# Attention scores and value products as full-precision small tiles inside a fused attention and MLP kernel

## The chip, the cores and the metric

The kernel runs on one core of one Trainium2 chip. The metric is the time of one execution on the device in microseconds (us). A run of it is some hundreds of microseconds of one program on five engines: PE (matmul; PEld is its weight load), DVE, ACT, POOL, and SP, which here only issues DMAs.

## What is computed

Attention with keys and values averaged over groups of 8 positions, then a two-layer MLP with a rational activation. 8 batches x 8 heads x 576 queries x 64; so 72 pooled keys for each head, 4608 tokens, 512 model columns, 2048 hidden columns, all float32:

```python
k_p = k.reshape(B, H, Sp, 8, D).mean(axis=3);  v_p = v.reshape(B, H, Sp, 8, D).mean(axis=3)
scores = scale * np.matmul(q, k_p.transpose(0, 1, 3, 2))
attn = softmax(scores)                               # over the 72 pooled keys
x = np.matmul(attn, v_p)  ->  (4608, 512)
h = x @ w_in;  g = P(h) / (Q(h) + 1e-6)              # cubic over quadratic, by element
out = g @ w_out
```

## The kernel before

**Blocks.** The tokens go through in 13 blocks: blocks 0 to 2 of 256 tokens ("short", `i < SHORT`) and 3 to 12 of 384 ("late"). 128 tokens are one tile `t`. A block of 384 lies in one batch (7 of the ten) or crosses from one batch into the next (3); `segs` gives its pieces.

**Attention of a block** (`attend`, L847). `squares` brings `q` in; `attention` (L712) runs once for each `t`: it makes `qT`, multiplies it by the pooled keys `kpT` into the scores `ps` (two PSUM banks), subtracts the maximum, takes the exponential on ACT, the sum on DVE, and normalises on POOL. The keys of the two heads of a pair stand block-diagonally in `kpT` (zeros elsewhere), so that one full-size product has 144 columns, two heads of 72. These products are in full float32, which PE runs as two records each. Where a tile crosses into another batch, its products are 64 output columns wide, alternately in the two halves of the array (`128*64` in the rows). The weights are then turned so that keys lie on partitions: in the short blocks by PE into `pm` and `pr`, in the late ones by 32x32 squares on DVE and 16 DMAs for each block (`am<-e`). Since the 144 keys of two heads don't fit in 128 partitions, the first 16 go separately (`rem`, `four`).

**Values** (`values`, L798). The turned weights are split into a high part `hi` and a rest `lo` (tile `am`), the pooled values into `vm` (high, rest) and `vr` (`split_v`, L664). For each of 4 head pairs and each piece of the block there are four products in the faster reduced type float32r; the result `pv` is copied to `x` as high part and rest.

**MLP.** `mm1` (L906) makes a hidden slice `ph` by 12 products of 384 columns, `rational` computes the activation on ACT, DVE and POOL (5 DVE and 6 ACT passes for each slice) into `gh` and `gl`, `mm2` (L967) adds 9 products of 512 columns into the output banks `po`, three for a late block. So PE alternates `ph` and `po`, and PSUM's 8 banks are shared by `po`, `ph`, the activation's `rp`, `ps` and `pv`.

**What sets the order.** Nothing is issued as it is written. Every call is recorded as an `Op` with a planner's own cost (`Plan.add`), given a due time, shifted by the table `LATER` (operation number to microseconds), and `Plan.solve` (L199) lays the operations on the engines, the earliest start first and, within `LOOK` of it, the earliest due. `Plan.issue` (L297) emits that order; all instructions of the plan therefore have the line L339. Where the plan leaves PE idle early on, it adds filler matmuls (L330): 512 columns into `idle` up to a marked operation, 256 columns of zeros into the next operation's own bank after it.

Of the kernel before, what the change touches and what calls it, by code (L numbers as in the profile page):

```python
# [101 lines left out]
class Op:  # L102
    __slots__ = ("eng", "cost", "port", "calls", "deps", "users", "bufs", "due", "wait",
                 "ready", "seq", "bytes", "early", "slack", "start", "end", "done", "lead", "keep",
                 "spare")


class Plan:
# [8 lines left out]
    LOOK = 0.02  # L117
# [21 lines left out]
    }  # L139
    HOLD = {}  # L140

# [13 lines left out]
    def add(self, eng, cost, calls, port=False, claims=(), bytes=0, early=40.0, after=()):  # L155
        op = Op()
        op.eng, op.cost, op.port, op.calls, op.bytes = eng, cost, port, calls, bytes
        op.early, op.slack, op.lead = early, self.slack, 0.0
        op.keep, op.spare = self.keep, 0
# [39 lines left out]
    def solve(self):  # L199
# [14 lines left out]
        port = bus = 0.0  # L214
        flights = [0.0] * 8
        done, order = 0, []
        while done < len(self.ops):
            best = None
            for e, cands in engs.items():
                pick = None  # L220
                opts = []
                for op in cands:
                    t = max(at[e], op.ready)
# [46 lines left out]
            at[op.eng] = op.end  # L270
            if op.port:
                port = op.end
# [24 lines left out]
    def issue(self):  # L297
# [8 lines left out]
        for op in self.order:  # L306
            if op.eng == "pe":
# [8 lines left out]
                else:  # L316
                    to = None
                    own = op.calls[0][1][0]
                    if own.tile.it is None and free is not None and op.start < self.HEAD_END:
                        to, one, first = own.tile.real(), self.zeros, True  # L320
                        to = to.rearrange("p a b -> p (a b)") if len(own.tile.shape) > 2 else to
                        to = to[:, 0:256] if op.start - free > 0.5 else None
# [35 lines left out]
def tile_pooled_attention_then_rational_moe(  # L358
# [24 lines left out]
    REM = 2 * SP - P  # L383
# [29 lines left out]
    pool("work4", 3)  # L413
# [14 lines left out]
    def pe(ns, calls, claims=(), after=()):  # L428
        return plan.add("pe", ns / 1000, calls, claims=claims, after=after)
# [23 lines left out]
    masks = new("cpool", "masks", [P, 6], F32, "masks")  # L453

    spread = new("work1", "vs", [P, 3 * P], F32, "fourfold")
    fourfold, line, ab = spread[:2 * REM, 0:P], spread[0:1, P:2 * P], spread[0:1, 2 * P:2 * P + 6]
    bands = new("cpool", "bands", [P, 4], F32, "bands")

    mlo, mhi = masks[:, 0:1], masks[:, 1:2]

    mrem_lo, mrem = ([masks[:, i + m:i + m + 1] for m in range(2)] for i in (2, 4))
# [6 lines left out]
    def make_masks():  # L468
        def band(m, lo, hi):

            small("memset", m, 1.0 / G)
            if lo > 0:
                small("affine_select", out=m, in_=m, pattern=[[0, 1]], compare_op=ALU.is_ge,
                      fill=0.0, base=-lo, channel_multiplier=1)
            if hi < P:
                small("affine_select", out=m, in_=m, pattern=[[0, 1]], compare_op=ALU.is_ge,
                      fill=0.0, base=hi - 1, channel_multiplier=-1)
# [11 lines left out]

# [644 lines left out]
```

## Time and profile before

| | |
|---|---|
| three runs | 883.92, 886.62, 886.92 us |
| median | 886.62 us |
| span of the profiled execution | 882.1 us |
| PE busy | 865.0 us, 98% |
| DVE, ACT, POOL busy | 770.0 (87%), 725.3 (82%), 549.7 us (62%) |
| matmuls of the MLP (`ph`, `po`) | 3936 of 5056 PE records |

The span reaches from the first to the last instruction; the median of the runs is 4.5 us above it. A PE record's duration includes the way through the array, which overlaps with the next record, so a cost is read as the distance between the starts of two groups, not as the duration of one.

### The profile page before, as it was taken

The numbers are of one execution on the slowest core, as the hardware profiler recorded it, in microseconds if no ns is written. First come the engines' busy times: TensorE is split into PE (matmuls) and PEld (weight loads), VectorE is DVE, ScalarE is ACT, GpSimd is POOL, SyncE is SP. The second block draws the span as 40 slices with busy tenths as digits, with TensorE's granted clock in tenths as the row PEclk, the third lists the DMA queues.
The fourth block names the chain that finished last, engine by engine and source line by source line (L and its number), as shares of the span: only waits on it lengthen the run. The fifth ranks groups of instructions, "written<-read, shape, count | busy, mean of one in ns | idle before, by whom it ended". The sixth has DMA issues, their size and how long they took to land.

```text
span 882.1 us, 15805 instructions
## 1 busy us (share of the span) xinstructions
PE 865.0 (98%) x5056; PEld 802.3 (91%) x5056; DVE 770.0 (87%) x1585; ACT 725.3 (82%) x1373; POOL 549.7 (62%) x614
## 2 busy tenths in 40 slices
PE   8899989999999999999999999999999999999998
PEld 7799879898999999999999999999999999999997
DVE  6899987878998988988998987998998987997764
ACT  4798898987688788788798797788888888888886
POOL 5767779786646744666655854646655764554554
PEclk9999999999999999999999999999999999999999
DMA  9896651133344232144034142043232432030000
GB/s 297 203 391 239 166 128 47 37 121 108 79 117 110 43 80 60 30 93 129 15 77 101 30 87 36 37 84 75 94 54 50 113 54 38 37 49 6 37 1 36
DMA packets 192919, 79.17 MB, mean 90 GB/s; under 512 B 169412, under 2 KB 169412, under 8 KB 192836
## 3 DMA queue, kind: packets, MB, share of 16 engines
q1 hardware_dynamic: 192836, 78.16, 34.1%
q8 instruction: 40, 0.66, 0.3%
q14 instruction: 43, 0.35, 0.1%
HBM read 52.17 MB, written 14.16 MB: 75 GB/s over the span
## 4 chain that ended last, share of the span: by engine, by line
PE 75%; ACT 9%; DMA 4%; DVE 4%; POOL 3%; SPq 2%; issue 2%; POOLq 0%; DVEq 0%; ACTq 0%
PE po L339 35%; PE ph L339 34%; PE ps L339 3%; PE pv L339 3%; SPq L339 2%; DMA rwin<-in_moe_w_in_dram 2%; DMA q<-in_q_dram 2%; ACT rp L339 1%; DVE t L339 1%; ACT r L339 1%; ACT t L339 1%; POOL gl L339 1%; ACT gh L339 1%; ACT hi L339 1%; ACT m_wout L339 1%
## 5 line engine op out<-in xcount | busy, mean ns | idle before, releaser
L339 PE MATMUL ph<-x,win 128*128 128x384 f32 (+1 forms) x2208 | 379.5, 320 | 1.2 <-POOL win L339 0.6
L339 PEld LDWEIGHTS ph<-x,win 128*128 128x128 f32 x2208 | 356.4, 189 | 12.2 <-PE po L339 0.9
L339 PE MATMUL po<-wout,gh 128*128 128x512 f32 x1152 | 300.2, 383 | 4.9 <-ACT gh L339 4.4
L339 POOL TENSOR_TENSOR w<-w,r 128x384 f32<-128x384 f32 (+2 forms) x186 | 196.3, 1056 | 148.2 <-ACT r L339 137.5
L339 POOL TENSOR_TENSOR gl<-t,gh 128x384 fp32r<-128x384 f32 (+2 forms) x186 | 201.3, 1084 | 127.4 <-ACT gh L339 89.5
L339 PEld LDWEIGHTS po<-wout,gh 128*128 128x128 f32 x1152 | 209.3, 189 | 29.9 <-ACT gh L339 6.5
L339 DVE SCALAR_TENSOR_TENSOR t<-t,abn,rp 128x384 f32<-128x384 f32 (+2 forms) x186 | 115.0, 620 | 58.8 <-ACT rp L339 57.6
L339 PE MATMUL po<-wout,gl 128*128 128x512 f32 x576 | 162.0, 382 | 0.7 <-POOL gl L339 0.7
L339 ACT ACTIVATE t<-ph,abn 128x384 f32<-128x384 f32 (+2 forms) x186 | 125.9, 678 | 35.2 <-DVE rp L339 13.0
L339 ACT ACTIVATE r<-w,abn 128x384 f32<-128x384 f32 (+2 forms) x186 | 133.0, 715 | 9.2 <-POOL gl L339 4.3
L339 ACT ACTIVATE rp<-w,cbias 128x384 f32<-128x384 f32 (+2 forms) x186 | 110.5, 594 | 30.8 <-POOL w L339 25.7
L339 DVE TENSOR_TENSOR t<-t,ph 128x384 f32<-128x384 f32 (+2 forms) x186 | 104.0, 560 | 19.3 <-ACT w L339 10.4
L339 PEld LDWEIGHTS po<-wout,gl 128*128 128x128 f32 x576 | 104.6, 189 | 12.4 <-POOL gl L339 2.1
L339 DVE SCALAR_TENSOR_TENSOR t<-t,abn,ph 128x384 f32<-128x384 f32 (+2 forms) x186 | 114.8, 618 | 1.2
L339 ACT ACTIVATE w<-ph 128x384 f32<-128x384 f32 (+2 forms) x186 | 92.3, 496 | 22.0 <-PE ph L339 17.6
L339 ACT CAST gh<-t 128x384 fp32r<-128x384 f32 (+2 forms) x186 | 95.9, 516 | 14.7 <-DVE t L339 9.7
L339 DVE SCALAR_TENSOR_TENSOR t<-rp,t 128x384 f32<-128x384 f32 (+2 forms) x186 | 104.4, 561 | 1.9
L339 DVE SCALAR_TENSOR_TENSOR rp<-w,rp 128x384 f32<-128x384 f32 (+2 forms) x186 | 105.2, 566 | 0.0
L339 ACT ACTIVATE rp<-rp 128x384 f32<-128x384 f32 (+2 forms) x186 | 91.0, 490 | 2.2
L339 POOL TENSOR_TENSOR e<-e,sm 128x576 f32<-128x576 f32 x36 | 42.9, 1203 | 29.8 <-DVE sm L339 28.7
L339 POOL TENSOR_TENSOR st_v<-st_v 128x256 f32<-128x256 f32 (+1 forms) x72 | 42.2, 596 | 7.5 <-DMA st_v<-in_v_dram 4.6
L339 PE MATMUL ps<-kpT,qT 128*128 128x144 f32 (+1 forms) x304 | 41.6, 290 | 0.3 <-DVE qT L339 0.3
(116 smaller groups left out, 876.2 us busy)
## 6 DMA issues: line engine op xcount, KB each, us to landing
am<-e SPq DMA_DIRECT2D x160, 72.0 KB, 2.4
rwin<-in_moe_w_in_dram SPq DMA_DIRECT2D x8, 1024.0 KB, 8.4
rwout<-in_moe_w_out_dram SPq DMA_DIRECT2D x8, 1024.0 KB, 11.6
out_dram<-ob SPq DMA_DIRECT2D x30, 256.0 KB, 2.5
st_k<-in_k_dram SPq DMA_DIRECT2D x24, 256.0 KB, 3.2
st_v<-in_v_dram SPq DMA_DIRECT2D x24, 256.0 KB, 2.7
q<-in_q_dram SPq DMA_DIRECT2D x112, 48.0 KB, 2.1
xd<-x SPq DMA_DIRECT2D x6, 512.0 KB, 13.8
```

Source lines behind the costliest of these rows:

```text
L339: getattr(engines[op.eng], name)(*map(value, args), **{k: value(v) for k, v in kw.items()})
```

## The change

The score products take 64 rows and 64 output columns each, one head and 64 tokens, over 72 keys; four of them stand in the four quarters of the array, the two heads of a pair in different row halves and different PSUM banks. The value products take 32 keys and 64 output columns: four head pairs in four row groups and four banks, two heads in two column halves. Both are full float32, two records each. Weights and values are no longer split (`hi`, `lo`, `vm`, `vr` are gone). Short blocks turn their weights by float32 products with the identity, 32 output columns wide, instead of PE's transpose. Late blocks are handled whole: one `attention_all` with 48 score products into four banks, 24 or 48 value products into four banks. The planner gets a switching cost `DRAIN` between kinds of PE tile (`mode`), a rule that holds PSUM banks for an operation that needs more than two (`waits`, `room`), a `LOOK` of 0.3, and a new `LATER` table of some 430 entries.

```diff
-    LOOK = 0.02
+    LOOK = 0.3
     LATER = {
-        83: -4, 85: -17, 95: 2, 105: -1, 119: 4, 139: 27, 172: 1, 196: 5, 290: 5, 332: 2, 355: 10,
...
+        1: 20, 4: -810, 9: -530, 14: -380, 25: -380, 26: -40, 27: -210, 28: -70, 29: -210,
...
+    DRAIN = 0.18
...
+            wide = min((op for op in engs["pe"] if op.due <= at["pe"] + self.SOON
+                        and op.ready <= at["pe"] + self.AHEAD and op.waits()),
+                       key=lambda op: op.due, default=None)
+            room = wide and sum(b.ring.tag == "ps" for b in wide.bufs)
...
+                    t = max(at[e] + (self.DRAIN if e == "pe" and op.mode != mode else 0.0),
+                            op.ready)
...
+                                if wide and op is not wide and not mine[0].sum:
+                                    n += room
...
-    pool("work4", 3)
+    pool("work4", 4)
...
     def prep_v_early(n):
+        for r in range(4):
+            for hh in range(2):
+                rows = v[n, 2 * r:2 * r + 2].rearrange("h (s t) d -> (h s) (t d)", t=G)
+                dma(128, early(n, 2)[r * HB:(r + 1) * HB].rearrange(
+                    "p (c h x) -> p c h x", c=2, h=2)[:, :, hh],
+                    rows[WINDOWS[hh]:WINDOWS[hh] + 2 * HB].rearrange("(c k) x -> k c x", c=2))
-        dma(1024, st, rows[:, REM:, :].rearrange("j r x -> r j x"))
...
+    def scores(i, out, qT, ms):
+        calls = []
+        for m in ms:
+            for j in range(NJ):
+                for ch in range(2):
+                    n = (tok0(i) + m * P + ch * D) // S
+                    for hh in range(2):
+                        rows = slice(hh * D, (hh + 1) * D)
+                        o = out(hh, m, j)
+                        calls.append(mm(o.tile_at(slice(ch * D, (ch + 1) * D)), qT(rows, m, j, ch),
+                                        kpT[n % 2][rows, j, :], True, True))
+        return calls
...
+            return [mm(o(r), pairs[:, r, WINDOWS[u]:WINDOWS[u] + HB], ident, True, True)
+                    for r in range(4)]
+        pe(232 * 4, [x for u in range(4) for x in turned(
+            lambda r: pm[r * HB:(r + 1) * HB, u, :], u)], claims=(mt,), mode=3)
...
+    def attention_all(i, mt, qs, es):
+        dve(NJ * size(i)).transpose(qs, qs)
+        cut = 512 // SP
+        parts = ((0, cut), (cut, NQ))
+        ps = [[bank(f"ps{i}_{hh}{x}", [P, q1 - q0, SP]) for x, (q0, q1) in enumerate(parts)]
+              for hh in range(2)]
+        pe(127 * NQ, every, claims=(es, mx, sm), mode=1)
+        for x, (q0, q1) in enumerate(parts):
+            for hh in range(2):
+                k = q1 - q0
+                dve(k * SP).tensor_reduce(out=mx[:, hh, q0:q1], in_=ps[hh][x], op=ALU.max,
+                                          axis=AX.X)
+                dve(k * SP).tensor_tensor(
+                    out=es[:, q0:q1, hh], in0=ps[hh][x],
+                    in1=mx[:, hh, q0:q1].unsqueeze(2).to_broadcast([P, k, SP]), op=ALU.subtract)
...
-                    terms = ((o, vh[:, j, :], h), (o, vl[:, j, :], h),
-                             (pv[:D, jj, r0:r1], vr[b % 2][:, j, :], rest),
-                             (o, vh[:, j, :], l))
...
+        pv = [bank(f"pv{i}_{r}", [P, n]) for r in range(4)]
+        for r0, r1, b in segs(tok0(i), n):
+            w = vw[b % 2]
+            for c in range(3):
+                for r in range(4):
+                    rows = slice(r * HB, r * HB + (HB if c < 2 else 2 * LAST))
+                    for hh in range(2):
+                        calls.append(mm(pv[r][hh * D:(hh + 1) * D, r0:r1], w[rows, 2 * c + hh],
+                                        mt[rows, 2 * c + hh if c < 2 else 4, r0:r1],
+                                        c == 0, c == 2))
+        pe(cost, calls, claims=[x_at(xs, 0, j)[0] for j in (0, 2)], mode=2)
```

How the order moves is shown at three places. In the rows, `ps_0_4377` is a bank `ps` and its number; x2 means two such instructions in a row.

First, PE at the scores of late block 6, before; `po` belongs to the block that is in the MLP at that time:

```order
L339 MATMUL po_0_2_3544<-wout_2498,gl_7_1_4319 128x512
L339 MATMUL ps_0_4377<-kpT_184,qT_4293 128x144 x2
L339 MATMUL po_0_0_4384<-wout_752,gh_0_0_4348 128x512
L339 MATMUL po_0_1_4388<-wout_752,gh_0_0_4348 128x512
L339 MATMUL po_0_2_4394<-wout_752,gh_0_0_4348 128x512
L339 MATMUL po_0_0_4384<-wout_752,gh_0_0_4348 128x512
L339 MATMUL ps_1_4400<-kpT_184,qT_4293 128x144 x2
```

and in the changed kernel, the start of the same block's scores:

```order
L397 MATMUL po_0_2_3692<-wout_2580,gl_7_0_4474 128x512
L397 MATMUL po_0_0_3677<-wout_2580,gh_7_1_4492 128x512
L397 MATMUL po_0_1_3681<-wout_2580,gh_7_1_4492 128x512
L397 MATMUL po_0_2_3692<-wout_2580,gh_7_1_4492 128x512
L397 MATMUL ps_00_4516<-kpT_592,q_4335 64x72
L397 MATMUL ps_10_4518<-kpT_592,q_4335 64x72
```

Twelve products in six or fewer groups among the `po` became 48 small ones in one group, into four banks (`ps_00`, `ps_10`, `ps_01`, `ps_11`); `po` matmuls stand on both sides.

Second, DVE behind those scores, before:

```order
L339 TENSOR_REDUCE mx_4390<-ps_0_4377 128x4
L339 SCALAR_TENSOR_TENSOR t_1_1_4301<-rp_1_1_4352,t_1_1_4301 128x384
L339 TENSOR_TENSOR e_4406<-ps_0_4377,mx_4390 128x2x144
L339 TENSOR_TENSOR t_2_0_4339<-t_2_0_4339,ph_2_0_4286 128x384
L339 TENSOR_REDUCE mx_4390<-ps_1_4400 128x4
```

and in the changed kernel (`t` and `rp` are the activation's tiles, `mx` and `e` the attention's, `ob` the output copy):

```order
L397 SCALAR_TENSOR_TENSOR t_1_1_4505<-t_1_1_4505,abn,ph_1_1_4442 128x384
L397 TENSOR_REDUCE mx_4578<-ps_00_4516 128x7
L397 TENSOR_REDUCE mx_4578<-ps_10_4518 128x7
L397 TENSOR_SCALAR ob_7_0_4584<-po_0_0_3677 128x512
L397 TENSOR_REDUCE mx_4578<-ps_01_4546 128x5
L397 TENSOR_REDUCE mx_4578<-ps_11_4548 128x5
L397 TENSOR_TENSOR e_4611<-ps_00_4516,mx_4578 128x7x72
L397 TENSOR_TENSOR e_4611<-ps_10_4518,mx_4578 128x7x72
L397 TENSOR_TENSOR e_4611<-ps_01_4546,mx_4578 128x5x72
L397 TENSOR_TENSOR e_4611<-ps_11_4548,mx_4578 128x5x72
L397 SCALAR_TENSOR_TENSOR t_1_0_4456<-t_1_0_4456,abn,rp_1_0_4575 128x384
```

The passes over the scores stood one by one between passes of the activation; now eight of them and one output copy stand in a row.

Third, PE in the opening, at the turning of block 1's weights, before:

```order
L339 MATMUL ps_1_495<-kpT_102,early_1_208 128x144 x2
L339 MATMUL ph_1_0_478<-x_385,win_460 128x256 x20
L330 MATMUL pm_575<-zero,identr 128x256 x23
L339 MATMUL pm_575<-identr,e_472 128x128 x4
L339 MATMUL pq_606<-identr,q_476 128x128 x4
```

and in the changed kernel (line L388 emits its fillers):

```order
L388 MATMUL idle<-identr 128x512 x5
L397 MATMUL ph_2_0_505<-x_398,win_480 128x256 x16
L388 MATMUL idle<-identr 128x512
L397 MATMUL pl_639<-identr,ks_166 128x128
L397 MATMUL ph_2_0_505<-x_398,win_480 128x256 x4
L397 MATMUL idle<-identr 128x128
L388 MATMUL pm_683<-zero,identr 128x256 x48
L397 MATMUL pm_683<-identr,e_558 32x128 x16
```

The place has 48 filler matmuls of zeros where it had 23, and the 512-column fillers, which ended earlier, now reach up to it. Over the program the 512-column fillers go from 23 to 54 and those of 256 columns from 47 to 48.

## Rows read from the trace of the kernel before

**Rows 1.** The page: span, busy time by engine, granted TensorE clock in 40 slices (tenths).

```profile
span 882.1 us, 15805 instructions
...
PE 865.0 (98%) x5056; PEld 802.3 (91%) x5056; DVE 770.0 (87%) x1585; ACT 725.3 (82%) x1373; POOL 549.7 (62%) x614
...
PEclk9999999999999999999999999999999999999999
```

**Rows 2.** Busy time by stretch; columns as its first line says.

```profile
core 0: us, PE busy (x) PEld busy (x) DVE busy (x) ACT busy (x) POOL busy (x), PEclk, DMA share, GB/s
0.00:50.00 50.00, 43.78 (x307) 38.30 (x308) 38.55 (x81) 31.30 (x59) 32.59 (x71) 1.00 0.91 266
50.00:100.00 50.00, 48.83 (x354) 45.38 (x353) 49.76 (x96) 42.98 (x68) 34.25 (x22) 1.00 0.75 277
300.00:500.00 200.00, 199.79 (x1132) 186.94 (x1131) 183.61 (x398) 166.38 (x331) 119.74 (x139) 1.00 0.31 70
500.00:700.00 200.00, 199.60 (x1118) 185.77 (x1118) 179.47 (x389) 165.74 (x328) 116.70 (x129) 1.00 0.31 67
```

**Rows 3.** Order of time on PE, late, a tile in two batches: start us, us, instructions.

```profile
692.08 0.38 PE L339 MATMUL po<-wout,gl 128*128 128x512 f32 x1
692.39 1.20 PE L339 MATMUL ps<-kpT,qT 128*64 128x144 f32 x16
693.52 0.48 PE L339 MATMUL po<-wout,gl 128*128 128x512 f32 x1
693.84 0.38 PE L339 MATMUL po<-wout,gh 128*128 128x512 f32 x1
```

**Rows 4.** The same view in the opening: fillers, scores of a whole tile, transposes.

```profile
2.52 4.43 PE L330 MATMUL idle<-identr 128*128 128x512 f32 x10
...
11.43 1.14 PE L339 MATMUL ps<-kpT,early 128*128 128x144 f32 x8
12.41 3.62 PE L339 MATMUL pvs<-early,identr 128*128 128x256 f32 x16
...
37.75 2.74 PE L330 MATMUL pm<-zero,identr 128*128 128x256 f32 x23
...
43.83 0.60 PE L339 MATMUL pm<-identr,e 128*128 128x128 f32 x4
44.27 0.38 PE L339 MATMUL pr<-identr,e 128*128 128x128 f32 x2
```

**Rows 5.** The same view at values, block in one batch.

```profile
388.81 0.49 PE L339 MATMUL pv<-hi,vm 128*128 128x384 f32 x2
...
389.46 0.81 PE L339 MATMUL po<-wout,gh 128*128 128x512 f32 x3
```

**Rows 6.** The same view at values, block in two batches; between them 31 more.

```profile
526.41 0.81 PE L339 MATMUL po<-wout,gl 128*128 128x512 f32 x3
527.06 0.36 PE L339 MATMUL pv<-hi,vm 128*128 128x192 f32 x2
...
530.42 1.26 PE L339 MATMUL po<-wout,gh 128*128 128x512 f32 x5
```

**Rows 7.** Groups on DVE by form: count, busy us, mean ns, idle before.

```profile
L339 DVE TENSOR_REDUCE mx<-ps 128x4 f32<-128x288 f32 x72 | 30.8, 438 | 2.0 <-PE ps L339 1.8
L339 DVE TENSOR_TENSOR e<-ps,mx 128x288 f32<-128x288 f32 x72 | 29.8, 443 | 0.1
L339 DVE TENSOR_TENSOR x<-pv,x 128x384 fp32r<-128x384 f32 x40 | 21.2, 552 | 4.5 <-ACT x L339 4.0
...
L339 DVE TENSOR_TENSOR am<-am,hi 128x768 fp32r<-128x768 f32 x20 | 19.7, 997 | 0.7 <-ACT hi L339 0.2
...
L339 DVE TENSOR_SCALAR ob<-po 128x512 f32<-128x512 f32 x13 | 8.9, 686 | 2.9 <-PE po L339 2.7
```

**Rows 8.** Groups on ACT by form, the same columns.

```profile
L339 ACT CAST x<-pv 128x384 fp32r<-128x384 f32 x40 | 18.0, 480 | 2.1 <-PE pv L339 2.0
L339 ACT CAST hi<-am 128x768 fp32r<-128x768 f32 x20 | 16.3, 830 | 0.1
```

More of the change, by code (lines that the diff above doesn't have):

```diff
@@ L104, with waits @@
                  "ready", "seq", "bytes", "early", "slack", "start", "end", "done", "lead", "keep",
-                 "spare")
+                 "spare", "mode")
+    def waits(self):
+        out = [b for b in self.bufs if not b.held]
+        return sum(b.ring.tag == "ps" for b in out) > 2 and all(
+            len(b.ring.free) >= sum(x.ring is b.ring for x in out) and b in b.ring.queue[:2]
+            for b in out if b.ring.tag != "ps")
 class Plan:
@@ L452, in tile_pooled_attention_then_rational_moe @@
     zero = real([P, 1], F32R, tag="zero", name="zero")
[L453 to L461, printed above, removed]
+    line = new("work1", "vs", [P, 3 * P], F32, "line")
+    line, ab = line[0:1, 0:P], line[0:1, 2 * P:2 * P + 6]
+    masks = new("cpool", "masks", [P, 2], F32, "masks")
+    mlast = [masks[:, m:m + 1] for m in range(2)]
     QC = 1.0 + 1e-6
@@ L596, in prep_k @@
             if n < 2 or c1 == 5:
-                turned = pe(109 * len(turns_), turns_)
+                turned = pe(109 * len(turns_), turns_,
+                            after=[o for o, _ in kpT[n % 2].tile.reads])
                 turned.lead = 1.5 if n > 2 else 0.0
@@ L664, in split_v @@
[L664 to L680 removed]
+        place = early(n, 1)[:, CW:CW + RW]
@@ L710, in squares, with __init__, tile_at, attention @@
         return qs
-    def attention(i, m, hi, lo, qs, es):
+    def scores(i, out, qT, ms):
[10 more added lines that the diff above has]
+        return calls
+    class Part:
+        def __init__(self, bank_, at):
+            self.bank, self.at = bank_, at
+        def tile_at(self, rows):
+            return self.bank[rows, self.at, :]
+    def attention(i, m, mt, qs, es):
         t = tok0(i) // P + m
@@ L738, in attention @@
-        pairs = es[:, :, m]
-        e = es[:, 0:NJ, m].rearrange("p j (h s) -> p j h s", s=SP)
-        mx = new("work2", "mx", [P, H], F32, f"mx{t}")
-        sm = new("work2", "sm", [P, H], F32, f"sm{t}")
-        scores = [bank(f"ps{t}_{c}", [P, 4, SP]) for c in range(2)]
-        calls = [mm(scores[c][r0:r1, 2 * jj:2 * jj + 2, :], qT[:, 2 * c + jj, r0:r1],
-                    kpT[n % 2][:, 2 * c + jj, :], True, True)
-                 for c in range(2) for jj in range(2) for r0, r1, n in sg]
@@ L758, in attention @@
-        ef = es[:, 0:NJ, m]
-        act(H * SP + 24).activation(ef, ef, AF.Exp, scale=D ** -0.5)
-        dve(H * SP).tensor_reduce(out=sm.rearrange("p (j h) -> p j h", h=2), in_=e, op=ALU.add,
-                                  axis=AX.X)
+        j0 = m * (NJ // 2)
+        qt = qs[:, j0:j0 + NJ // 2].rearrange("p a b (c d) -> p (a b c d)", d=HB).rearrange(
+            "p (h d) -> p h d", d=D)
+        for r0, r1, n in sg:
+            s0 = t * P + r0 - n * S
+            dma(2 * (r1 - r0), qt[r0:r1],
+                q[n, :, s0:s0 + (r1 - r0), :].rearrange("h s d -> s h d"), run=256)
@@ new lines, in attention @@
+        pq = bank(f"pq{t}", [P, NJ, P])
+        pe(110 * NJ, [
+            ("transpose", (pq[:, j, :],
+                           qt[:, 2 * j:2 * j + 2, :].rearrange("s h d -> s (h d)"), ident),
+             {}) for j in range(NJ)], claims=(qT,))
+        act(NJ * P).copy(qT, pq)
+        e = es[:, m]
+        mx = new("work2", "mx", [P, 2, NJ], F32, f"mx{t}")
+        sm = new("work2", "sm", [P, H], F32, f"sm{t}")
+        ps = [bank(f"ps{t}_{hh}", [P, NJ, SP]) for hh in range(2)]
+        pe(127 * NJ, scores(i, lambda hh, m, j: Part(ps[hh], j),
+                            lambda rows, m, j, ch: qT[rows, j, ch * D:(ch + 1) * D], [m]),
+           claims=(e, mx, sm), mode=1)
@@ new lines, in attention @@
+        for hh in range(2):
+            dve(4 * SP).tensor_reduce(out=mx[:, hh], in_=ps[hh], op=ALU.max, axis=AX.X)
+            dve(4 * SP).tensor_tensor(
+                out=es[:, m, :, hh], in0=ps[hh],
+                in1=mx[:, hh].unsqueeze(2).to_broadcast([P, NJ, SP]), op=ALU.subtract)
+        act(H * SP + 24).activation(e, e, AF.Exp, scale=D ** -0.5)
+        normal(e.rearrange("p j h s -> p (j h) s"), sm, H * SP)
+        pm = bank(f"pm{t}", [P, 4, P])
+        pr = bank(f"pr{t}", [P, P])
@@ L843, in x_at @@
         return tile, idx if c is None else (idx[0], c, *idx[1:])
-    prepared, shared = set(), {}
+    prepared = set()
     def attend(i):
@@ L1060, in due @@
         return HEAD + SLOW * min(at, SLOWS) + PACE * max(0, at - SLOWS)
-    for i in range(2):
-        plan.add("pool", 0.5, [("memset", (kpT[i], 0.0), {})], port=True)
     plan.idle = bank("idle", [P, 4, P])
@@ L1069, in tile_pooled_attention_then_rational_moe @@
     plan.now = 0.0
-    for g in range(4):
-        small("tensor_copy", out=fourfold[:, g * 32:(g + 1) * 32], in_=ident[:2 * REM, :2 * REM])
     make_masks()
```

304 lines of the change are left out of this document (102 added, 202 removed), and 62 rows, old and new, of the table LATER.

## The prediction

> **What bounds the kernel now.** I read the page first: PE is busy 98% of 882.1 us and its clock is granted in full in every slice [rows 1], so the question is whether PE waits anywhere and what it spends on attention. By stretches [rows 2] there are two regimes. In the first 100 us PE is busy 43.78 and 48.83 of 50 us, that is 7.4 us idle, although it also runs fillers that produce nothing; there the DMA engines are busy for 91% and 75%. From 300 to 700 us PE idles 0.6 of 400 us: every microsecond of PE work taken out there comes off the end, and nothing that relieves another engine can bring anything, because nothing keeps PE waiting. DVE is next with 363 of the same 400 us, so it may become the bound if it is handled badly. Second view: the order of time on PE, read start to start [rows 3 to 6], since a record's duration overlaps with the next.
>
> **Paces.** A full-width score tile has 8 records from 11.43 to 12.41 us, 0.1225 us each [rows 4]; with 144 columns that is 0.85 ns a column in full float32. A `po` record of 512 columns takes 0.216 us (three from 526.41 to 527.06 [rows 6]), 0.42 ns a column in float32r: full precision costs twice. A tile in two batches already uses half-width products, alternately in the two column halves [rows 3]: 16 records in 1.20 us. The last record's own way is 0.28 us (1.14 less 7 spacings of 0.1225 [rows 4]), so 15 spacings take 0.92 us, 0.061 us each, half the full-width spacing: two tiles do run side by side. The price stands at both ends. `po` at 692.08 would have let the array go at 692.30, and the next regular rhythm begins at 693.84 - 0.216 = 693.62; that is 1.33 us for 16 records which need 0.98. An excursion into small tiles costs 0.35 us.
>
> **Late blocks, scores.** Now: 3 tiles x 0.98 = 2.94 us a block, and 0.35 more in the three blocks with a tile in two batches. Then: 48 products, 96 records, four side by side, is 24 sets of 72 columns x 0.85 ns = 0.061 us, 1.47 us, and one excursion: 1.82. Saved: 7 x 1.12 + 3 x 1.47 = 12.2 us.
>
> **Late blocks, values.** Now 0.65 us a head pair (388.81 to 389.46 [rows 5]), 2.60 a block in one batch, and 3.36 in two (527.06 to 530.42 [rows 6]). Then 24 products, 48 records, eight side by side: 6 sets x 384 x 0.85 ns = 1.96 us, or 12 sets of 192 columns, also 1.96, and an excursion: 2.31. Saved: 7 x 0.29 + 3 x 1.05 = 5.2 us. That row groups work side by side like column halves is not in this trace; I take it so for now and price the contrary below. Together the late blocks give **-17.4 us**, all on the path by the 0.6 us idle [rows 2].
>
> **Late blocks, other engines.** The split of the weights goes: two passes of 997 ns and a half-height one on DVE, copies of 830 ns on ACT for each block [rows 7, 8]. The normalised weights go out in 16 DMAs as before, a sixth smaller. Since PE does not wait there, I cost all this at nothing; it is slack for the last rival.
>
> **Short blocks.** Six score tiles: from 5 x 0.98 + 1.33 = 6.2 us to 6 x (0.49 + 0.35) = 5.0, -1.2. Turning the weights: 36 records at 0.11 us (four from 43.83 to 44.27 [rows 4]), 4.0 us, become 240 float32 records, four side by side, 60 x 128 x 0.85 ns = 6.5 us, and five excursions, 1.75: +4.3. The values of three blocks change by less than a microsecond and are left out. The net is +3.1 us.
>
> **Fillers.** The order has 31 more of 512 columns. Four more stand in the first group, which runs at 0.44 us each (ten in 4.43 us [rows 4]); 27 at 0.216; that is 7.6 us. The zeros of 256 columns go from 47 to 48, at 0.12 us (23 in 2.74 us [rows 4]), no term, but 48 of them now stand in one place. Fillers stand where the plan expects PE to wait. If they only cover the 7.4 us that PE idles in the first 100 us [rows 2], they cost nothing; if all of that idle stays, they cost 7.6. Neither row is nearer, so I take half, +3.8, and keep both ends. The value loads of batches 0 and 1 become 12 DMAs each instead of 3; four of the first eight, 0.5 MB, stand ahead of the first `q`, 2 us at 266 GB/s [rows 2]. I hold that within the fillers' term.
>
> **Sum.** -17.4 + 3.1 + 3.8 = -10.5 us. This is made against the profiled execution of 882.1 us and carried to the median of the runs, 886.62, which lies 4.5 above it: **876 us**. Its own range is 868 (fillers free, cheaper excursions, since neighbouring ones share an end) to 881 (fillers in full).
>
> **Rival 1: small records do not keep up.** A set of four score records must start at 15 ns each, against 61 ns, the closest sustained spacing in any row here [rows 3]. For the forecast: there the array sets the spacing (each column half gets a record every 122 ns, exactly the full-width pace), so 61 is no sign of a limit on starts. Against it: no row shows anything denser, and none shows two row groups at once. Priced as a lowest spacing f: 1152 score records planned at 15 ns, 288 value records at 20, 96 at 14, 96 at 27, 336 at 41, 240 turning records at 27. At f = 25 ns they cost 13.7 us more, 890; at 61 ns, 87 us more, 963. Row groups that wait for one another, so that a set of scores takes twice and one of values four times as long, give 18 + 70 us, also about 963. The change stops paying at f = 24.
> The Trainium skill speaks against this change here: "TensorE: Matmul & The Clock Gate", section "Wait — 56ns, not 53.3ns?", says that matmul starts never lie closer than about 25 ns, and that with hardware decode off a matmul costs 62 ns of the sequencer. By the first the kernel would come to 890, by the second to 963, both estimates from that page. The 61 ns of the split tile would fit the second as well as the array; that pairs keep exactly half the full-width pace speaks for the array.
>
> **Rival 2, slower: four banks at once.** `po` holds three of the eight PSUM banks, and scores or values now take four in one step, so one is left for `ph` and `rp`. Behind block 6's scores DVE has eight score passes and an output copy in a row. From 443 ns for 288 columns and 552 for 384 [rows 7], 1.14 ns a column, a pass of 504 takes 0.69 and one of 360 0.53: 4.9 us, with the copy of 0.69 5.5 us, in which no activation pass runs except on ACT and POOL. PE has 15 to 21 `po` records ready behind most of these places, 3.2 to 4.5 us, and then needs a bank and later new `gh`. It would wait 1.0 to 2.3 us, taken as 1.5, ten times. At values the banks come free after 0.48 + 4 x 0.55 = 2.7 us [rows 7, 8] with 6 to 15 `po` records, 1.3 to 3.2 us, ahead: 0.5, ten times. That is +20 us, 896 (to 913 at the high ends). It decides above a mean wait of 0.53 us at each of the 20 places. Against it: the place already exists in small (0.6 us idle in 400 with four value banks in quick turn), DVE loses about 3 us a block, and a freed bank lets PE run `ph` first.
>
> **Rival 3: the opening ends later.** If the fillers come on top in full (+3.8) and the idle of the opening doubles, because scores start 2 us later and each block's weights are turned by longer products (+7.4), it gives 887. For it: 91% DMA share in the first 50 us [rows 2] leaves no room for loads in a worse order. Against it: chains there lose the split passes.
>
> **Chances.** Forecast 0.58, rival 1 0.12, rival 2 0.14, rival 3 0.16. About 0.5%, 4.4 us, is what a measurement of this kernel tells from no change: faster is below 882, slower above 891. Nearly all of the forecast is faster, with a little of rivals 2 and 3: 0.58 in all. Rival 3, the edge of the forecast and rival 1 at 25 ns make "same": 0.19. Most of rivals 1 and 2 make "slower": 0.23. The range reaches down to 867 and up to 902, which leaves out rival 1 beyond 32 ns and the dear half of rival 2, some 0.17.
>
> **What would show it.** Score records in sets of four within 61 ns and 24 sets in 1.5 us: the late saving is right; starts at even spacings of 25 ns or more: rival 1. About 0.35 us of array time lost for each of some 30 excursions: the switching price. PE idle from 300 to 700 us above 5 us, in front of `ph` or `po` and behind DVE passes over the scores: rival 2. PE's first 100 us: idle below 3 us says that the fillers replaced waiting, above 10 us is rival 3; the hundredth `ph` record compared with before tells how much later the opening ends. The forecast is wrong if the sum of `ps` and `pv` starts to starts does not fall by some 17 us after the short blocks.

## The result, and the profile after

The changed kernel takes 876.21 us (median of 5 runs, 875.04 to 880.71), the kernel before 884.43 beside it (883.92 to 886.92): a ratio of 0.9911, 95% interval 0.9885 to 0.9937. The profiled spans are 873.1 and 882.1 us [rows 1]. So the forecast time, 876.0, was met; but the runs of before came out 2.2 us lower than those the sum started from, so the saving is 8.2 us by the medians (7.9 by the ratio) and not 10.5, and the steps below show that errors of both signs stand in it. Two of the five runs of the changed kernel lie near 880 us; the traces compared below are those of the fastest run of each kernel (875.04 and 883.92).

The page of the changed kernel, its span, busy times and granted clock, against [rows 1]:

```profile
span 873.1 us, 18781 instructions
...
PE 859.9 (98%) x6668; PEld 778.7 (89%) x6668; DVE 747.8 (86%) x1399; ACT 691.5 (79%) x1281; POOL 534.1 (61%) x560
...
PEclk9999999999999999999999999999999999999999
```

Busy time by stretch, against [rows 2]:

```profile
0.00:50.00 50.00, 46.81 (x502) 38.98 (x506) 34.71 (x74) 26.13 (x40) 27.71 (x33) 1.00 0.91 251
50.00:100.00 50.00, 47.02 (x691) 39.89 (x684) 43.29 (x82) 39.49 (x60) 31.22 (x20) 0.97 0.86 300
300.00:500.00 200.00, 199.25 (x1478) 181.14 (x1478) 178.56 (x351) 158.91 (x309) 119.69 (x136) 1.00 0.29 65
500.00:700.00 200.00, 199.82 (x1483) 182.03 (x1482) 178.92 (x347) 161.34 (x316) 119.46 (x137) 1.00 0.29 65
```

PE stays the bound: it idles 0.93 us from 300 to 700 us, and DVE is busy 357 us there instead of 363. In the first 100 us PE idles 6.2 us instead of 7.4, and the clock of 50 to 100 us is 0.97: it was granted at half (1.2 GHz) from 55.12 to 58.53 us, half a microsecond after a wait of PE for a load had ended at 54.59. The order of time on PE, as in [rows 3 to 6]: scores of an early late block, scores of two others, values.

```profile
81.35 0.59 PE L397 MATMUL po<-wout,gh 128*128 128x512 f32 x2
81.88 1.73 PE L397 MATMUL ps<-kpT,q 64*64 64x72 f32 x96
83.54 0.70 PE L397 MATMUL po<-wout,gh 128*128 128x512 f32 x2
...
284.92 2.37 PE L397 MATMUL ps<-kpT,q 64*64 64x72 f32 x96
287.21 0.91 PE L397 MATMUL po<-wout,gl 128*128 128x512 f32 x3
...
687.51 2.52 PE L397 MATMUL ps<-kpT,q 64*64 64x72 f32 x96
689.97 0.70 PE L397 MATMUL po<-wout,gl 128*128 128x512 f32 x2
...
450.89 2.19 PE L397 MATMUL pv<-am,vw 32*64 32x384 f32 x48
453.02 0.48 PE L397 MATMUL po<-wout,gl 128*128 128x512 f32 x1
```

From its first record to the next `po`, a group of 96 score records takes 1.66 us in blocks 3 and 4 (81.88 to 83.54), but 1.78 to 2.45 in the other eight; values take 2.12 to 2.14 in eight blocks, 2.44 and 2.83 in the other two. A group's whole cost is a little more, since the `po` records on both sides stand further from it than their 0.216 us. It is taken here from where the `po` ahead would have let the array go to where the rhythm behind begins, the way the forecast read 1.33 us off [rows 3].

**Where the time went.** The ledger below compares both traces. The late blocks' groups are summed by that whole cost. For the opening I count the MLP work begun by a given time, each `ph` and `po` record at its array time: the changed kernel is 6.7 us behind at 100 us, 6.6 at 110 and 8.8 ahead at 860. At 110 us both have done the same attention work.

| step | forecast, us | measured, us | from |
|---|---|---|---|
| late scores | -12.2 | -10.5 | 31.9 (30 tiles, three split) to 21.4 (1.86 to 2.65 a block) |
| late values | -5.2 | -5.0 | 29.3 to 24.3 (2.32 a block, but one 2.64 and one 3.03) |
| opening: short blocks and fillers | +6.9 | +7.7 | 6.6 behind at 110 us, although block 3's scores, done by then, had gained 1.1 |
| a wait of PE for `gh` at 117 us is gone | none | -3.3 | the row below |
| not traced to a place | none | +2.3 | what is left over |
| sum | -10.5 | -8.8 | spans: -9.0 |

The longest waits of PE, of the kernel before and then of the changed one (us in all, times, longest):

```profile
PE po L339 <- ACT gh L339: 4.4, 3, 3.1
```

```profile
PE pq L397 <- DMA q<-in_q_dram: 2.2, 1, 2.2
PE idle L397 <- DVE identr L1118: 1.8, 1, 1.8
PE ph L397 <- issue: 1.0, 1, 1.0
```

The first of before was a stall of the MLP behind the opening. The changed kernel has none there, and none either without its table of due times (e6): so it is not the table that removes it. Whether the planner's other rules do, or the later opening, which gives the activation time to catch up, no run shows. I had not priced it.

### The profile page after: what moved, and what is told of

Its sections match the earlier page's. It is cut to its first block, busy times and chain, and to the rows that moved or that the text cites. A ratio compares the mean times of both kernels' runs of the same rounds, so it can differ in the third digit from the quotient of the medians.

```text
span 873.1 us, 18781 instructions
## 1 busy us (share of the span) xinstructions
PE 859.9 (98%) x6668; PEld 778.7 (89%) x6668; DVE 747.8 (86%) x1399; ACT 691.5 (79%) x1281; POOL 534.1 (61%) x560
## 4 chain that ended last, share of the span: by engine, by line
PE 82%; SPq 6%; DVE 4%; DMA 3%; ACT 2%; issue 2%; POOL 1%; DVEq 0%; POOLq 0%; ACTq 0%
PE po L397 38%; PE ph L397 37%; SPq L397 6%; PE pv L397 3%; PE ps L397 2%; DVE t L397 2%; DMA q<-in_q_dram 1%; DMA early<-in_v_dram 1%; ACT rp L397 1%; PE pvs L397 1%; DMA early<-in_k_dram 1%; DVE rp L397 0%; PE pm L397 0%; PE pvr L397 0%; DVE st_k L397 0%
## 5 line engine op out<-in xcount | busy, mean ns | idle before, releaser
L397 PE MATMUL ph<-x,win 128*128 128x384 f32 (+1 forms) x2208 | 369.4, 320 | 0.2
L397 PE MATMUL po<-wout,gh 128*128 128x512 f32 x1152 | 296.7, 381 | 1.7 <-DVE t L397 0.7
L397 POOL TENSOR_TENSOR gl<-t,gh 128x384 fp32r<-128x384 f32 (+2 forms) x186 | 194.9, 1050 | 131.2 <-ACT gh L397 98.7
L397 PEld LDWEIGHTS po<-wout,gh 128*128 128x128 f32 x1152 | 211.4, 189 | 31.9 <-DVE t L397 1.6
L397 ACT ACTIVATE t<-ph,abn 128x384 f32<-128x384 f32 (+2 forms) x186 | 124.0, 673 | 13.1 <-PE ph L397 5.2
L397 ACT CAST gh<-t 128x384 fp32r<-128x384 f32 (+2 forms) x186 | 95.9, 517 | 18.1 <-DVE t L397 12.2
L397 POOL TENSOR_TENSOR e<-e,sm 128x864 f32<-128x864 f32 (+1 forms) x26 | 39.6, 1538 | 39.0 <-DVE sm L397 34.2
L397 POOL TENSOR_TENSOR st_v<-st_v 128x256 f32<-128x256 f32 (+1 forms) x60 | 36.7, 620 | 9.6 <-DMA st_v<-in_v_dram 8.9
L397 PEld LDWEIGHTS ph<-xr,win 128*128 128x128 f32 x288 | 36.1, 191 | 2.5 <-issue 1.2
## 6 DMA issues: line engine op xcount, KB each, us to landing
rwin<-in_moe_w_in_dram SPq DMA_DIRECT2D x8, 1024.0 KB, 10.5
```

Source lines behind the costliest of these rows:

```text
L397: getattr(engines[op.eng], name)(*map(value, args), **{k: value(v) for k, v in kw.items()})
```

## The experiments

**Do row groups really work side by side?** Only the order of the products inside a group is changed: scores by head first, values by row group first.

```diff
-        for m in ms:
-            for j in range(NJ):
-                for ch in range(2):
-                    n = (tok0(i) + m * P + ch * D) // S
-                    for hh in range(2):
+        for hh in range(2):
+            for m in ms:
+                for j in range(NJ):
+                    for ch in range(2):
+                        n = (tok0(i) + m * P + ch * D) // S
...
-            for c in range(3):
-                for r in range(4):
+            for r in range(4):
+                for c in range(3):
```

> Only the order in which the products of a group are issued changes: scores first for all of head one (rows 0 to 63), then for all of head two; values first for one group of 32 rows, then the next. Two column halves still stand next to each other, row groups no longer do. Theory (the late gain comes from row groups at work side by side): the 96 score records of a late block go from 1.66 to about 3.1 us, the 48 value records from 2.12 to about 8 us, the short blocks in proportion; some 18 us more for scores and 70 us for values, about 963 us in all. Rival (what set the gain is only the smaller amount of data, the order within a group does not matter, since small products are started ahead wherever a tile is free): 1.66 and 2.12 us stay, 876 us.

Measured: 904.62 us, span 902.6. Scores and values of one block:

```profile
428.70 3.03 PE L397 MATMUL ps<-kpT,q 64*64 64x72 f32 x96
431.67 0.70 PE L397 MATMUL po<-wout,gh 128*128 128x512 f32 x2
...
464.03 4.28 PE L397 MATMUL pv<-am,vw 32*64 32x384 f32 x48
468.24 0.48 PE L397 MATMUL po<-wout,gl 128*128 128x512 f32 x1
```

Scores take 2.97 us, as the theory said. That is 48 pairs of 0.061, and side by side it is 1.66. So the order decides, and row groups do work at once. But values take 4.2 us and not 8. The records show why: in the group at 464.03 the second row group's first records start at 464.74, ahead of six records of the first row group that stand before them in the program and start from 465.05 to 465.71. A record that waits for its own tile does not hold back those for other tiles; with 12 records to a row group, two row groups can be at work, and 4.2 us is half of 8. With 48 (scores) the run-ahead seen here would not reach the other row group, and 2.97 us agrees. The forecast of 963 was wrong by this.

**What does changing the tile size cost?** Six whole-array products of zeros, overwritten by what follows, among the 48 score products of each late block (e2), or all ahead of them (e3, with `every.insert(0, ...)`).

```diff
+for n, at in enumerate((4, 12, 20, 28, 36, 44)):
+    o = out(0, at // 16, at // 4 % 4)
+    every.insert(at + n, mm(o.bank[:, o.at, :], identr, zero.to_broadcast([P, SP]), True, True))
```

> Six products of zeros over the whole 128x128 array (72 columns, two records of 0.061 us each) are put among the 48 score products of each of ten late blocks, one after every eighth; the score products that follow overwrite them. Beside it e3, with the same six ahead of the group. Theory (an excursion into small tiles costs 0.35 us whatever stands in it): against e3 six more excursions in ten blocks, +21 us; against the changed kernel 7 us more for the products themselves, +28 us, about 904. Rival (the 0.35 us was read off two places where something else was late; changing the tile size only breaks the overlap of neighbours, 0.05 to 0.1 us): +3 to +6 us against e3, 886 to 889.

> The same six products of zeros for each of ten late blocks, all ahead of the 48 score products, where the array still works as a whole. Both theories: 12 records of 0.061 us in ten blocks, 7.3 us more than the changed kernel, about 883; it is what e2 is compared with.

Measured: 898.67 and 884.46 us, a difference of 14.2. The same block in e2, then in e3:

```profile
427.56 0.30 PE L397 MATMUL ps<-zero,identr 128*128 128x72 f32 x1
427.79 0.48 PE L397 MATMUL ps<-kpT,q 64*64 64x72 f32 x16
428.20 0.30 PE L397 MATMUL ps<-zero,identr 128*128 128x72 f32 x1
428.43 0.48 PE L397 MATMUL ps<-kpT,q 64*64 64x72 f32 x16
428.84 0.30 PE L397 MATMUL ps<-zero,identr 128*128 128x72 f32 x1
```

```profile
422.23 0.75 PE L397 MATMUL ps<-zero,identr 128*128 128x72 f32 x6
422.91 1.85 PE L397 MATMUL ps<-kpT,q 64*64 64x72 f32 x96
```

In e2 the rhythm is 0.64 us for 16 score records (four sets, 0.245) and one product of zeros (0.114, six in 0.68 us in e3). So an excursion costs 0.28 us, far above 0.1 and somewhat under the 0.35 of the forecast. The difference in time is less than 60 x 0.28 = 17 because in e3 the groups of blocks 5 to 12 lose up to 0.8 us to the waits of e9 (2.45 in blocks 3 and 4, up to 3.27 us whole), which e2's even 4.20 us hide: the ten groups together differ by 14.8.

**What do the fillers cost?** e4 leaves out the 48 products of zeros (the first pair of lines), e5 also the 512-column fillers planned after 9 us (40 of the 54).

```diff
-    HEAD_END = 60.0
+    HEAD_END = 0.0
-                if op.start <= steady:
+                if op.start <= min(steady, 9.0):
```

> The 48 products of zeros with 256 columns that stand in the opening in one group are left out, nothing else. They take about 5.8 us of the array. Theory (fillers stand where PE would wait, so half of them is cover): the time falls by 2 to 3 us, to about 873.5. Rival A (all cover, PE idles in their place): 876, within 1 us. Rival B (they keep the clock up; without them the products that follow run at the half rate): 1 to 5 us longer.

> The products of zeros are left out, and the fillers of 512 columns planned after 9 us too; only the first group stays. Theory (half of the fillers is cover): 4 to 6 us shorter than the changed kernel, 870 to 872. Rival A (all is cover): 876, with PE idle in the first 100 us up by 10 us or more. Rival B (the clock falls in the gaps): longer than 876, with a granted clock of the first 100 us below 0.9.

Measured: 879.25 us, ratio to before 0.993 (0.9911 to 0.995), and 878.5 us, 0.9932 (0.9914 to 0.9951). Neither is faster than the changed kernel with 0.9911. The place in the changed kernel, then in e4:

```profile
44.10 5.62 PE L388 MATMUL pm<-zero,identr 128*128 128x256 f32 x48
49.78 2.19 PE L397 MATMUL pm<-identr,e 128*32 128x128 f32 x64
51.79 0.62 PE L397 MATMUL pr<-identr,e 128*32 128x128 f32 x16
54.59 0.63 PE L397 MATMUL pq<-identr,q 128*128 128x128 f32 x4 [2.18 <-DMA q<-in_q_dram]
```

```profile
43.19 0.39 PE L397 MATMUL idle<-identr 128*128 128x128 f32 x2
49.01 3.64 PE L397 MATMUL pm<-identr,e 128*32 128x128 f32 x64 [5.44 <-POOL e L397]
52.42 1.08 PE L397 MATMUL pr<-identr,e 128*32 128x128 f32 x16
```

Without zeros PE waits 5.44 us for the normalised weights of block 1, almost exactly as long as the zeros ran. PE comes out of the wait at half clock, and the turning takes 3.41 us (49.01 to 52.42) instead of 2.01. So the zeros cover a wait whole and also keep the clock; e5's first 100 us have a granted clock of 0.93 and 0.89, and PE idles 13.7 us more in them. So rival A's idle and rival B's lower clock are both there (e5's mean of 0.91 just misses the 0.9 that B named), and the theory of half is wrong.

**Is it one late load?** e7 moves only block 2's query loads forward in SP's queue.

```diff
+moved = [x for x in o if x.eng == "sp" and named(x, "q2")]
+for x in moved:
+    o.remove(x)
+at = max(n for n, x in enumerate(o) if x.eng == "pe" and named(x, "pq3")) + 1
+o[at:at] = moved
```

> Only the order of issue on SP changes: the DMAs that bring block 2's turned queries stand right behind the transposes of block 3's, ahead of other loads. In the changed kernel PE waits 2.2 us for them at 52.4 us, and the clock stands at half from 55.05 to 58.46 us, which costs the short score and value groups there about 1.6 us. Theory (both losses come from those DMAs standing in the queue behind others): wait and half rate go, 2 to 4 us shorter, 872 to 874. Rival (what is moved back in the queue, block 3's queries and value pieces, is now late by as much): 875 to 878, with a new wait for a DMA between 50 and 70 us.

Measured: 876.87 us, ratio 0.9915 (0.9895 to 0.9936), no difference. The wait is gone and the clock of 50 to 100 us is 1.00, but PE waits elsewhere for other engines:

```profile
PE pm L397 <- POOL e L397: 1.8, 1, 1.8
...
PE pq L397 <- DVE x L397: 1.4, 1, 1.4
PE pvr L397 <- DVE e L397: 1.1, 1, 1.1
```

The rival was right, except that PE meets the late loads through passes: on DVE the transpose of block 3's queries now waits 1.68 us for its own loads, with block 1's small passes queued behind it.

**Shorten that chain by order alone (e8).** `hoist` takes steps of one engine out of the finished plan and puts them right behind what they need; ScalarE's pass on a weight load (`m_wout1`) goes behind the copies `am1`, and 16 zeros stay of 48.

```diff
+hoist("sp", "q2", pq3[-1:])
+for name in "sm2", "sm3":
+    hoist("dve", name, (), ("tensor_scalar", "reciprocal"))
+hoist("pool", "e1")
+hoist("dve", "am1")
+hoist("act", "am1")
...
+hoist("act", "qT4")
+for c in range(2):
+    hoist("act", f"x1_{c}")
+    hoist("dve", f"x1_{c}")
```

> The opening's chain is shortened by order alone, no work is left out but 32 of the 48 products of zeros: behind the second block's exponentials DVE takes the four small passes on their sums (sm) at once, ahead of the 1.78 us transpose of block 3's queries and of 2 us of other passes; GpSimd normalises right behind them; the copies of the turned weights (am) stand on ScalarE ahead of a pass that waits for a weight load until 50.85 us; the value results (x) stand ahead of weight preparation; block 2's queries are loaded earlier as in e7. Theory (what the opening loses is the wait for the second block's normalised weights, 43.9 to 49.8 us, which the zeros only hide): turning starts at about 46 us and not at 49.8, the first po record comes 3 to 4 us earlier than 73.1 us, 872 to 873 us in all. Rival (the opening is set by the DMA engines, busy 91% there): turning starts earlier but another wait for a DMA takes its place, first po at 72 to 73 us, 875 to 877.

Measured: 879.78 us, ratio 0.9929 (0.9915 to 0.9943), no faster than the changed kernel, and its span is 877.4 us against 873.1. DVE, then GpSimd:

```profile
43.89 3.53 DVE L397 TENSOR_SCALAR sm<-sm 128x8 f32<-128x8 f32 x1
47.46 0.20 DVE L397 RECIPROCAL sm<-sm 128x8 f32<-128x8 f32 x1
```

```profile
44.58 0.44 POOL L397 TENSOR_TENSOR ks<-early 64x128 f32<-64x128 f32 x1
44.99 2.40 POOL L397 TENSOR_TENSOR wout<-m_wout,wout 128x1024 fp32r<-128x1024 f32 x1
```

The small pass, 0.16 us in the changed kernel, took 3.53 and ended (47.42) with GpSimd's pass (47.39). e10, which has the same order, shows it again (3.53 us, ending 0.03 us after GpSimd's pass). Moved forward, it ran into GpSimd's work, by these two traces; that is not so for every DVE pass, since a sum of 128x8 in the changed kernel took its usual 0.75 us (43.18) beside the same pass of GpSimd (42.08 to 44.50). Turning began at 49.42 instead of 49.78, and PE met new waits (2.0 us for GpSimd's `ks`) and half clock (0.90). This refutes my new order, not the chain as the cause.

**Waits inside the group (e9).** Two products that read a piece of every part of the queries stand ahead of the 48 and take the waits for their 16 loads.

```diff
+for hh in range(2):
+    o, rows = out(hh, 0, 0), slice(hh * D, (hh + 1) * D)
+    every.insert(hh, mm(o.tile_at(slice(0, D))[:, 0:4 * NQ], kpT[0][rows, 0, 0:D],
+                        qs[rows, 0:NJ, :, 0:1].rearrange("p j b s -> p (j b s)"), True, True))
```

> In the ten late blocks two products of 48 columns, which read a piece of every part of the block's queries, are put ahead of the 48 score products, which overwrite them; so all waits for the 16 loads of the queries are taken there, and none is left between the score products. Theory (the sets of four break where an instruction waits on a semaphore in the middle of the group, though it has long been set): the groups of blocks 5 to 12, now 1.78 to 2.45 us, come to 1.66 plus 0.1 to 0.2 us each, and the sum of the ten falls from 19.4 to about 18; the time falls by 1 to 1.5 us. Rival (the time of the groups depends on something else, or taking the waits costs the same wherever it is done): the groups stay at 1.9 to 2.5 us with the first records spread out, 876 to 878.

Measured: 875.23 us. The same two blocks as above:

```profile
286.49 0.28 PE L397 MATMUL ps<-q,kpT 64*64 64x48 f32 x2
...
288.29 0.70 PE L397 MATMUL po<-wout,gl 128*128 128x512 f32 x2
...
688.32 0.28 PE L397 MATMUL ps<-q,kpT 64*64 64x48 f32 x2
...
690.12 0.70 PE L397 MATMUL po<-wout,gl 128*128 128x512 f32 x2
```

Both take 1.80 us instead of 2.29 and 2.46, and so do the others but one (2.00); the sum of the ten falls from 19.4 to 18.2. The loads had landed long before, so the waits cost time by being there. Seen from the end, 1.2 us is less than the scatter of single runs, and 875.23 is one run; its clock was at half from 67.62 to 71.03 us, and its MLP stood 0.9 us behind the changed kernel's at 110 us.

> e8 and e9 in one kernel. The two places are apart (before 75 us and behind 80 us), so the gains add: 870.5 to 872 us if both theories hold; 876 if neither; near e8 if the waits cost the same in front of the group.

The two edits together: 878.64 us, ratio 0.9916 (0.9898 to 0.9933). The late groups are at 1.80 to 1.89, and the opening has e8's loss.

**What does the table of due times bring?** Emptied in the changed kernel, and in the kernel before (there also without fillers for narrow banks):

```diff
-    LATER = {
...
+    LATER = {}
```

> The changed kernel with its table of due times emptied, so that the planner orders everything by its own rules; the tiles are the same. Theory (the gain is the array time of the tiles, 17 us in the late blocks, and the table only repairs waiting in the first 100 us): late blocks keep 1.7 and 2.1 us for scores and values, PE idles under 3 us from 300 to 700 us, and the opening loses up to 10 us, 877 to 887 in all. Rival (the new order is what keeps PE from waiting for banks when scores take four at once): PE idles over 10 us from 300 to 700 us, about 896.

> The kernel before with its own table of due times emptied (and no filler where a bank is narrower than a filler), for comparison with the changed kernel without its table (889.9 us). Theory (the tiles gain 17 us in the late blocks whatever the table, and each table repairs waits that its own order has): 895 to 905 us, 5 to 15 us above the changed kernel without table. Rival (the gain comes from the new order): about 885 to 890, no better and no worse than the changed kernel without table.

Measured: 889.94 and 892.37 us. Both kernels lose, the changed one 13.7, the one before 7.9 (one run each). The changed kernel without its table, from 300 us:

```profile
300.00:500.00 200.00, 197.36 (x1465) 1.00 0.29 65
500.00:700.00 200.00, 195.15 (x1444) 1.00 0.29 65
```

PE idles 7.5 us there instead of 0.9, mostly `ph` waiting for DVE (4.2 us, 9 times). But the kernel before without its table idles 3.9 us there instead of 0.6, so what taking four banks at once can have added is at most 3.6 us; each table removes most waits of its own kernel. Without tables the changed kernel, with its tiles and its planner's new rules, is 2.4 us ahead, less than the 5.7 us over which its own five runs scatter: neither theory nor rival.

**The loads of the opening (e11).** In the changed kernel block 1's queries wait for block 0's value staging to come free; the value products begin at 17.05 us (12.41 before [rows 4]), the second query load leaves SP at 33.39 us (24.76 before), block 1's last scores start at 39.43 (33.66), and the turning of its weights at 49.78 (41.13). So the delay grows by another 2.9 us between scores and turning, where the changed kernel's small passes on the sums stand behind a transpose on DVE. The row of before:

```profile
41.13 0.66 PE L339 MATMUL pm<-identr,e 128*128 128x128 f32 x4 [0.65 <-POOL e L339]
```

In both kernels SP's issues wait, from the ninth on, for the load eight places before. So I joined the twelve value loads of a batch into five: eight of 32 x 2 x 512 became four of 4 x 32 x 512, and four of 32 x 512 one. The query loads and fillers change as the expectation says.

```diff
+        rows = v[n].rearrange("(r h) (s t) d -> r (h s) (t d)", r=4, t=G)
+        for at in range(4):
+            whole.append((parts[0][at::2] if at < 2 else parts[1][at - 2::2], early(n, 2)[
+                :, at * RW:(at + 1) * RW], rows[:, WINDOWS[at % 2] + at // 2 * HB:][:, :HB]))
+        whole.append((parts[2], early(n, 1)[:, CW:CW + RW],
+                      rows[:, WINDOWS[4]:WINDOWS[4] + HB]))
...
+    for ops, dst, src in whole:
+        first = min(ops, key=o.index)
+        for x in ops:
+            if x is not first:
+                o.remove(x)
+        first.calls = [("dma_start", (dst, src), {})]
```

> The values of batches 0 and 1 come in 5 loads each over all 128 partitions instead of 12 over 32; block 1's two query loads go one behind the other ahead of block 3's, block 2's as in e7; 12 of the 48 products of zeros and about a third of the 512-column fillers after 12 us are left out; the late blocks take their waits first, as in e9. Theory (each load on SP is issued only when the one eight before it has landed, so 12 small loads a batch push back everything behind them: block 0's values at 17.05 us, block 1's second query load at 33.39 us, its second scores at 39.43, its turned weights at 49.78): value sums begin by 15 us, the second query load is issued by 26 us, block 1's last scores come by 37 us and the turning by 47; the first po record by 70.5 us instead of 73.1, and 871 to 873 us in all. Rival (the place is set by passes on DVE and GpSimd, as e8 suggests): the loads come earlier but turning starts at 49 to 50 us as before, PE waits there where fillers were, 875 to 878 us, less 1 for the late blocks.

Measured: 893.11 us, ratio 1.0085 (1.0064 to 1.0106), slower than before. PE's waits, its stretches, and its place at the values:

```profile
PE pvs L399 <- DMA early<-in_v_dram: 7.5, 1, 7.5
PE pvs L399 <- DMA early<-in_k_dram: 5.2, 1, 5.2
```

```profile
0.00:50.00 50.00, 38.86 (x404) 0.86 0.77 210
50.00:100.00 50.00, 38.64 (x483) 0.86 0.74 230
```

```profile
25.93 5.17 PE L399 MATMUL pvs<-early,identr 128*128 128x256 f32 x12 [5.17 <-DMA early<-in_k_dram]
30.94 1.89 PE L399 MATMUL pvr<-early,identr 128*128 128x64 f32 x16
```

Fewer loads came later, not sooner. One issued at 12.72 us landed from 13.71 to 21.23 us, 8.5 us for 256 KB, with 5 landing records where the others leave 16; the DMA share falls to 0.77. In the changed kernel a load of half that size, issued at 8.88, landed at 15.21, 6.3 us later. The Trainium skill ("DMA: Bandwidth & Descriptors", section "Why a DMA increments its semaphore by 16 and not by 1") says that such a load is spread over the largest number of engines, up to 16, that divides the slowest dimension of both sides, and that the engines left out are counted at once: with my 4 x 32 x 512 that is 4 engines and 5 records, and the trace has 5. So this run does not test its theory (earlier loads), but something near the reverse: value products begin 8.9 us later, another wait of 7.5 us comes at batch 1's, and the span is 18.3 us longer. By 110 us the MLP is 18.9 us behind the changed kernel, and it stays 15 to 20 behind. What the opening loses, the end loses. How much of it the spread over engines cost is not shown: the clock of the first 100 us fell to 0.86, and the order of the query loads and the fillers were changed too.

## Why the prediction was right, and where it was not

- **Late values: right**, 2.32 us a block against 2.31 in eight of the ten, eight products side by side; two took 2.64 and 3.03, and no run shows why. So was the pace of small score records: blocks 3 and 4 cost 1.86 us whole against 1.82. The four records of a set start 6 to 7 ns apart, sets every 62.5 ns, and 96 records take 1.66 us. That refutes rival 1 (by whose own counts the change would have stopped paying at 23 ns, not 24). The Trainium skill's floors ("TensorE: Matmul & The Clock Gate", section "Wait — 56ns, not 53.3ns?"), about 25 ns between starts, or 62 with hardware decode off, do not hold here for records on different tiles: 15.6 ns are sustained.
- **The switching price: right to 0.07**: 0.28 us inside a group (e2), and 0.36 to 0.39 around a whole one (values 2.32 less 1.96, scores 1.86 less 1.47), against 0.35.
- **Late scores: mis-sized.** The term held for blocks 3 and 4; in the other eight the waits for the query loads' semaphores stand among the products and break the sets, 1.78 to 2.45 us instead of 1.66. The forecast's step "96 records is 24 sets" left out that these products carry waits. e9 took them out and got 1.80 everywhere but once. By its own sign (the sum of `ps` and `pv` falls by some 17 us) the forecast got 15.5.
- **Opening: the size was right, the reason wrong.** The forecast took +3.1 of longer turning and half of 7.6 us of fillers as array time. e4 and e5 show that leaving fillers out gains nothing that can be measured: what they cover is longer, and the clock falls without them. Between 43.9 and 49.8 us PE has, in this order, nothing to do but wait for block 1's normalised weights, whatever runs there. The step that failed is "fillers, +3.8"; in its place stands later data, 4.6 us at the value products, 5.8 at block 1's last scores and 8.7 at the start of its turning. I had named the loads, "four of the first eight ... 2 us", and put them inside the fillers' term. e11 shows that what an opening falls behind (18.9 us at 110 us) is still missing at the end (18.3 us of span). That the loads are the cause, and that bringing them earlier would give the time back, is argued, not shown, since no run made the delay shorter. Of the longer turning I can't say how much shows.
- **Rival 2: refuted for this kernel** by 0.93 us of idle in 400, with the order that its table plans; without the table it is 7.5 us (e6), far below the 20 us of the rival, and 3.9 us for the kernel before. The argument that `ph` runs first in a freed bank was not tested.
- **Rival 3: half right**: the hundredth `ph` record starts at 68.4 us instead of 57.4, about the rival's 11.2 us, though idle did not grow and the MLP is only 6.6 us behind by 110 us; its time, 887, was not met.
- **Missed:** the 3.3 us wait for `gh` at 117 us, which pays for more than the scores (1.7) and the opening (0.8) together fell short of; another 2.3 us is lost late and not traced. That the time still came out at 876 is luck in part: the errors of the terms cancel down to a saving 2.3 us short of the forecast, and the runs of before came out 2.2 us lower.

## What to carry to other kernels

Small full-precision tiles pay at a bound TensorE if each group fills all tiles in turn, is entered once, and carries no semaphore wait inside: take the waits on a product in front. A filler is priced by what comes behind it, so leave it out and look before counting its array time as a cost. In an opening where the DMA engines are 91% busy, look at when the first data of each block lands, and at how a load is spread over the engines, before its count.

## What the runs showed of the hardware that I had not expected

- Records run ahead of others that stand before them in the program if their tile is free (e1, by six records). The Trainium skill says otherwise: "TensorE: Matmul & The Clock Gate", section "Step-by-step: what each phase is for", has matmuls start in program order.
- A DVE pass over 128x8 elements took 3.53 us instead of 0.16 while GpSimd worked, at the end on 128x1024 (e8, and again e10).
- A load of 4 x 32 x 512 left 5 landing records where others leave 16, and took 8.5 us for 256 KB (e11).
- One wait of PE does not tell what the granted clock will do: it fell to half after a wait of 2.2 us (changed kernel, from 55.12 us) and after one of 1.6 (e4, from 68.17), but not after one of 1.8 (e7), nor after the 3.1 us of the kernel before (full from 112 to 126 us).
